# A hand-written scheduler's table of durations, and one PSUM ring for scores and sums: an attention, channel-mix and MLP kernel

## The chip, the cores and the metric

The kernel runs on one core of a Trainium2 chip. The metric is the device time of one execution in microseconds (us), lower is better. Three runs of the kernel before gave 2530.54, 2530.79 and 2534.72 us, median 2530.79. One further execution was recorded by the hardware profiler; all rows below are from that one.

## The reference

Three stages follow one another, all in float32 (cut to what matters):

```python
scores = (1 / S) * z @ z.T                  # per batch: B, S, D = 4, 3072, 256; z has 64 columns
x = u * (np.maximum(scores, 0) ** 2 @ v)
x_prev = x shifted by one row
r = sigmoid((mu_r * x + (1 - mu_r) * x_prev) @ w_r)
x = r * (np.maximum((mu_k * x + (1 - mu_k) * x_prev) @ w_k, 0) ** 2 @ w_v)
out = np.maximum(x @ w_in, 0) ** 2 @ w_out
```

The last line is the second MLP on the rows of the second stage. The change touches only the first stage, the attention.

## The kernel before, in words

The attention (`attention()`, L411 to L885) works in 24 blocks of 512 query columns, 6 per batch, numbered `n`; `ib` is the block's number in its batch. A block runs over 24 steps `s` of 128 keys, in 6 groups `g` of 4 steps. In each step TensorE multiplies the values (`vhl`, a high and a low part) with the squared scores (`ahi`, `alo`, again a high and a low part) and adds to four PSUM banks: two halves of 128 output rows (`d` = 0, 1), each kept in two banks because two matmuls of 64 rows run side by side (`attend_mm`, L678). A step is 12 matmuls.

The scores are symmetric. For `g >= ib` TensorE computes a pair of score tiles (`score_pair`, L581) into two PSUM banks; ScalarE takes relu into a tile `a` (L593) and squares it (L598); ScalarE or VectorE casts the high part (`high`, L615, the cast is in a helper at L240); VectorE subtracts for the low part (`low`, L622). For `g > ib` VectorE also transposes the tile in 32x32 blocks into `turn` (L556), and after four of them a DMA stores it (`store_turned`, L559). The blocks with `g < ib` load these stored tiles back (`load_turned_scores`, L568) instead of computing them. `spread[ib, g]` is true for `ib >= 2`: there the transpose writes and reads with another order of its axes.

At a block's end the four sums are copied out of PSUM (`gate`, L735): `gate_part` copies one bank into `x` (L716), `gate_rest` the other into `rest` or `a` (L721), `gate_add` adds them, `gate_mult` multiplies by the transposed `u` (`turn_u`, tile `uT`, one buffer for each `d`), and `gate_store` sends the product to DRAM (L733). The two last steps of a block do `d` = 0 first, and the first step of the next block begins with its `d` = 0, so that the first two banks have 1.36 us (two steps' `d` = 1 part) to be copied out. In between, TensorE also issues the score pairs of the steps up to seven ahead.

The order in which each engine gets its instructions is made on the host by `Plan` (L22 to L170), a list scheduler. Each operation is a node with an engine (P, V, S, D for TensorE, VectorE, ScalarE and DMA; some may go to S or V), a cost and what it depends on. TensorE's order is fixed, and it gives the due times: a node's due time is that of whoever depends on it, less a lag (L84 to L90). `run` then plays time forward: each engine takes, of the nodes that are ready and have their buffers, the one due first. Buffers are rings (`take` reserves one, `use` adds a reader); a buffer is free when the last reader has ended by the plan's own clock. `MARGIN` scales the costs for each engine, `lead` says how long before its due time a load may start. The chip does not see the plan's times: each engine works its queue in the planned order and waits on semaphores. A DMA is issued by SP's queue, which is also in order.

In the plan before, all DMA issues take 0.1 us of the queue (L151), a transpose of scores costs 0.63, and the first matmuls of a block name the copies of the last block's sums as their dependences (L698):

```python
before = get("acc", d) if s % NJ == 0 and 0 in terms else ()
...
i = on_pe(attend_mm, s, d, ks, deps=(x, *v_nodes(b, g, c // 2), *(before or ())), cost=0.2267 * len(ks))
```

Score tiles have a ring `w` of four PSUM banks, the sums four banks of their own (`ps_d`).

Of the kernel before, what the change touches and what calls it, by code (L numbers as in the profile page):

```python
# [8 lines left out]
F32 = mybir.dt.float32  # L9
# [12 lines left out]
class Plan:  # L22
# [6 lines left out]
    def __init__(self, **rings):  # L29
        self.nodes, self.takes, self.users_of, self.last = [], {}, {None: []}, {}  # L30
        self.held = {k: [None] * n for k, n in rings.items()}
        self.beside = {}
        self.place, self.tiles, self.turns, self.lines = {}, {}, dict.fromkeys(rings, 0), {}
# [28 lines left out]

    def load(self, f, *a, deps=(), cost=4.5, lead=1e9):
        return self.node("D", cost, lambda e: f(*a), *deps, lead=lead)

# [7 lines left out]
    def run(self, **free):  # L73
# [43 lines left out]
        while waiting or pe:  # L117
            best = None
            slots = [(i, t) for i in waiting if (t := slot(i)) is not None]
            for e in "PVSD":  # L120
                if e == "P":
                    cand = [(pe[-1], t)] if pe and not missing[pe[-1]] and (t := slot(pe[-1])) is not None else []
                else:
                    cand = [(i, t) for i, t in slots if e in nodes[i][0]]
                if not cand:
                    continue
                start = max(free[e], min(t for _, t in cand))
                rank = lambda i: nodes[i][4] + self.BEHIND_CASTS * (e + nodes[i][0] == "VSV")
                i = min((i for i, t in cand if t <= start), key=lambda i: (rank(i), i))
                if self.ahead and e in "VS":  # L130
                    end = start + self.cost_on(i, e) * self.MARGIN[e]
                    soon = [(rank(k), k, t) for k, t in cand if start < t < end - 0.1 and rank(k) < rank(i) - 1.0
                            and nodes[k][4] + late < end + self.ahead]
                    if soon:
                        first = min(t for _, _, t in soon)
                        fits = [k for k, t in cand if t <= start and start + self.cost_on(k, e) * self.MARGIN[e] <= first + 0.1]
                        if fits:
                            i = min(fits, key=lambda i: (rank(i), i))
                        else:
                            start = first  # L140
                            i = min((k for k, t in cand if t <= start), key=lambda i: (rank(i), i))
                if best is None or start < best[0]:
                    best = start, e, i
            start, e, i = best
            if e == "P":
                pe.pop()
                late = max(late, start - self.due_of[i])
            else:
                waiting.remove(i)
            took = self.cost_on(i, e) * self.MARGIN[e]  # L150
            free[e] = start + (took if e != "D" else 0.1)  # L151
            ended[i] = end = start + took
# [21 lines left out]
def tile_relu2_attention__rwkv_channel_mix__relu2_mlp(  # L174
# [236 lines left out]
    def attention():  # L411
        with ExitStack() as st:
# [3 lines left out]
            FIRST, LEAD, WHOLE = 4, 7, 2  # L416
            ps_s = st.enter_context(tc.tile_pool(name="ps_s", bufs=4, space=PSUM))
            ps_d = st.enter_context(tc.tile_pool(name="ps_d", bufs=1, space=PSUM))
            z_raw, zT, zz, zhi, zlo, vhl, uT = {}, {}, {}, {}, {}, {}, {}
            plan = Plan(a=4, hi=LEAD + 1, lo=LEAD + 1, w=4, zn=2, zT=1, turn=2, mixed=3, raw=3, vhl=NG, zz=NG // 2,  # L420
                        uT0=1, uT1=1, rest=1, e=1, m=1)
# [4 lines left out]
                          "lo": [io.tile([P, T], F32R, tag="alo", name="alo", bufs=LEAD + 1) for _ in range(LEAD + 1)],  # L426
                          "w": [ps_s.tile([P, T], F32, tag="w", name="sps") for _ in range(4)],
                          "zn": [io.tile([P, T], F32, tag="zn", name="zn") for _ in range(2)],
# [47 lines left out]
            def z_nodes(b, g):  # L476
# [3 lines left out]
                if b:  # L480
                    ready = take(load(load_z, b, g, cost=5.0, lead=60.0, deps=(get("zload"),)), "zn", key)
                    last["zload",] = ready
# [4 lines left out]
                else:  # L487
                    ready = last["zn", g] if g == 1 else take(load(load_z, b, g, cost=4.5, lead=14.0), "zn", key)
                    ready = take(use(on_pe(turn_z, b, g, deps=(ready,), cost=0.3), key), "w", ("zps", g))
# [24 lines left out]
            def v_nodes(b, g, h):  # L514
                if ("vn", b, g, h) in last:
                    return last["vn", b, g, h]
                if h == 0:
                    if b or g:
                        last["v", b, g] = take(load(load_v, b, g, cost=5.5, lead=40.0 if b else 14.0), "raw", ("v", b, g))
                        take(last["v", b, g], "vhl", ("vhl", b, g))  # L520
                    before = last["v", b, g]
                else:
                    before = v_nodes(b, g, 0)[0]
# [107 lines left out]
            def turned_nodes(n, g):  # L631
                key, b = ("ready", n, g), n // NB
                first = take(node("D", 0.01, lambda e: place_turned(n, g), last["stored", b, g, n % NB], lead=45.0),
                             "mixed" if n < NBLK - 1 else "zz", key)
                last[key] = [use(load(load_turned_scores, n, g, k, deps=(first,), cost=5.5), key) for k in range(R)]

            def scores(s):
# [27 lines left out]
                if g > ib:  # L665
                    key = "turn", b, ib, g
                    v_ = use(on_v(turn, s, ib, g, c, deps=(q, get(*key)), cost=0.63), ("rel", s))
                    plan.beside[v_] = last["at", s][1], 0.5
# [5 lines left out]
                    if c == G - 1:  # L674
                        reads = get("ready", (b - 1) * NB + g, ib) or ()
                        last["stored", b, ib, g] = use(load(store_turned, ib, g, deps=(v_, *reads), cost=5.5), key)

            def attend_mm(s, d, terms):  # L678
# [3 lines left out]
                if first and terms[0] == 0:  # L682
                    acc[n, d] = [ps_d.tile([P, T], F32, tag=f"v{d}{i}", name=f"v{d}") for i in range(2)]
                ds_ = slice(d * P, (d + 1) * P)
# [11 lines left out]
            def attend(s, d, terms):  # L696
                n, b, ib, g, c = chunk(s)
                before = get("acc", d) if s % NJ == 0 and 0 in terms else ()  # L698
                hi, lo = last["at", s]
                if s < WHOLE:  # L700
                    use(on_pe(attend_mm, s, d, terms, deps=(hi, last["v", 0, 0], *(before or ())), cost=0.85), ("whole", s), ("v", 0, 0))
                    return
                for part in ((0, 1), (2,)):
                    ks = tuple(k for k in terms if k in part)
                    if ks:
                        x, key = (lo, "lo") if 2 in part else (hi, "hi")
                        i = on_pe(attend_mm, s, d, ks, deps=(x, *v_nodes(b, g, c // 2), *(before or ())), cost=0.2267 * len(ks))
                        last["mm", d] = use(i, (key, s), ("vhl", b, g))

# [25 lines left out]
            def gate(n, d):  # L735
                ld = take(load(load_u, n, d, cost=4.5, lead=30.0), "zn", ("u", n, d))
                tr = take(use(on_v(turn_u, n, d, deps=(ld,), cost=0.63), ("u", n, d)), f"uT{d}", ("uT", n, d))
# [13 lines left out]
                last["mult", d] = last["mult", n, d] = m  # L751
                last["acc", d] = p, r
                last["xT", n, d] = use(load(gate_store, n, d, deps=(m,), cost=3.0), ("uT", n, d))

# [31 lines left out]
            last["zn", 1] = node("D", 5.0, lambda e: None)  # L786
            mu_loaded = load(load_mu, lead=100.0)
            om_made = on_v(make_om, deps=(mu_loaded,), cost=0.15)
# [40 lines left out]
            for i, (src, done, rests) in enumerate(conversions):  # L829
# [5 lines left out]
                k0, total = sum(ops[:i - mine[0]]), sum(ops)  # L835
                p = take(load(load_raw, key, src, src.shape[1], src.shape[2], cost=6.0, lead=8.0), "raw", key)
                for k, f in enumerate(convert(key, done, rests)):
# [34 lines left out]
            for k, (n, which, c) in enumerate([(n, w, c) for n in range(2) for w in range(2 - n) for c in range(ND)]):  # L872
                if (which, c) == (0, 0):
                    ld = load(load_x, n, deps=[*(last["xT", n, d] for d in range(ND)), *blends], lead=25.0)
                    blends = []
# [6 lines left out]
                use(on_v(mixed, n, which, c, True, deps=(hi,), due=due + 3), key)  # L882
            plan.MARGIN = {"P": 1.0, "V": 1.0, "S": 1.0, "D": 1.0}
            plan.ahead = 1.0
# [837 lines left out]
```

## Time and profile before

| what | value |
|---|---|
| median of three runs | 2530.79 us |
| the profiled execution | 2529.5 us |
| its span, first to last instruction | 2527.7 us |
| TensorE busy | 2474.2 us (98%) |
| VectorE busy | 2091.2 us (83%) |
| ScalarE busy | 1798.9 us (71%) |
| mean granted TensorE clock | 0.993 |
| end of the attention (last matmul on `vhl`) | about 984 us |

A busy engine is not one at its limit, so the idle stretches of TensorE are read next to its granted clock: a stretch with a clock of 0.5 costs twice the time for the same matmuls. A wait names the engine that waited, its line, and what ended the wait. In a timeline, a line stands for some instructions of one kind in a row; the bracket at its end is the idle time of that engine before it.

### The profile page before, as it was taken

The page shows a single profiled execution, that of the slowest core. Times are in us where ns is not written, and L with a number is a line of the kernel's source. Part 1 is how long each engine was busy: PE and PEld are TensorE (multiplying, and loading weights), DVE is VectorE, ACT ScalarE, POOL GpSimd, SP SyncE. Part 2 cuts the span into 40 slices and gives each one's busy share as a digit, 9 for nine tenths or more (in the row PEclk, how much of TensorE's full clock was granted, in tenths as well). Part 3 has the DMA queues.
Part 4 walks back from the last instruction along what each step waited for, and adds up shares of the span by engine and source line. Part 5 has one row for each costly group of instructions (what it writes and reads, how often), then busy time and mean ns, then how long its engine had stood idle before and what let it go on. Part 6 is the DMA issues. An engine that isn't in the chain of part 4 may idle for free.

```text
span 2527.7 us, 39583 instructions
## 1 busy us (share of the span) xinstructions
PE 2474.2 (98%) x14721; PEld 2044.2 (81%) x14721; DVE 2091.2 (83%) x3473; ACT 1798.9 (71%) x3266; POOL 0.7 (0%) x6
## 2 busy tenths in 40 slices
PE   9989999999999999999999999999999999999998
PEld 6878887788778778888888888888888888888887
DVE  8878887898788787999999998877777777777776
ACT  8756875686578666888888887666666666666665
POOL 0000000000000000000000000000000000000000
PEclk9999999999999999999999999999999999999999
DMA  8667566666657654232232211100110011100100
GB/s 221 180 192 197 179 196 177 170 196 197 190 160 216 187 162 138 80 104 80 82 106 80 88 67 59 34 17 17 34 34 17 17 34 34 30 22 17 34 17 18
DMA packets 309442, 257.95 MB, mean 102 GB/s; under 512 B 205312, under 2 KB 224768, under 8 KB 306176
## 3 DMA queue, kind: packets, MB, share of 16 engines
q1 hardware_dynamic: 307136, 254.89, 34.3%
q8 instruction: 115, 1.88, 0.3%
q10 hardware_dynamic: 2112, 0.52, 0.1%
q14 instruction: 79, 0.65, 0.1%
HBM read 149.45 MB, written 105.91 MB: 101 GB/s over the span
## 4 chain that ended last, share of the span: by engine, by line
PE 85%; DVE 6%; DMA 3%; ACT 2%; SPq 2%; issue 2%; DVEq 0%; ACTq 0%
PE ups L1135 26%; PE v L693 21%; PE v L1151 10%; PE v L1153 10%; PE v L1152 10%; PE ups L369 3%; PE sps L586 3%; DVE alo L622 3%; SPq L438 1%; DMA xT<-uT 1%; DVE turn L556 1%; ACT a L593 1%; ACT a L598 1%; DMA raw<-in_moe_w_v_dram 0%; SPq L573 0%
## 5 line engine op out<-in xcount | busy, mean ns | idle before, releaser
L693 PE MATMUL v<-ahi,vhl 64*128 64x512 f32 x4592 | 729.4, 392 | 28.9 <-DVE x L240 12.8
L693 PEld LDWEIGHTS v<-ahi,vhl 64*128 64x128 f32 x4592 | 525.2, 187 | 118.4 <-DVE x L240 17.3
L693 PE MATMUL v<-alo,vhl 64*128 64x512 f32 x2296 | 476.0, 392 | 9.1 <-DVE alo L622 9.0
L1172 ACT ACTIVATE s<-s 128x512 f32<-128x512 f32 x288 | 180.8, 628 | 324.2 <-DVE s L1167 324.2
L693 PEld LDWEIGHTS v<-alo,vhl 64*128 64x128 f32 x2296 | 301.0, 187 | 55.9 <-DVE alo L622 16.0
L1151 PE MATMUL v<-hhi,wout 128*128 128x512 f32 x768 | 299.0, 389 | 0.0
L1153 PE MATMUL v<-hlo,wout 128*128 128x512 f32 x768 | 299.0, 389 | 0.0
L1152 PE MATMUL v<-hhi,wout 128*128 128x512 f32 x768 | 299.0, 389 | 0.0
L1135 PE MATMUL ups<-d,win 128*128 128x512 f32 x1056 | 296.6, 389 | 0.0
L1184 DVE TENSOR_TENSOR hlo<-s,hhi 128x512 fp32r<-128x512 f32 x384 | 264.5, 689 | 16.5 <-ACT hhi L240 1.0
L593 ACT ACTIVATE a<-sps 128x512 f32<-128x512 f32 x335 | 192.8, 610 | 96.6 <-PE sps L586 47.0
L1176 ACT ACTIVATE s<-s 128x512 f32<-128x512 f32 x384 | 231.4, 628 | 6.1
L1167 DVE TENSOR_TENSOR s<-ups,su 128x512 f32<-128x512 f32 x192 | 131.4, 684 | 122.8 <-PE ups L1135 122.8
L1135 PEld LDWEIGHTS ups<-d,win 128*128 128x128 f32 x1056 | 198.3, 188 | 41.1
L1135 PE MATMUL ups<-b,win 128*128 128x512 f32 x792 | 222.4, 389 | 0.0
L556 DVE STREAM_TRANSPOSE turn<-a 128x512 f32<-128x512 f32 x240 | 206.0, 862 | 15.0 <-ACT a L598 7.8
L622 DVE TENSOR_TENSOR alo<-a,ahi 128x512 fp32r<-128x512 f32 x334 | 215.5, 677 | 2.5 <-ACT ahi L240 0.6
L598 ACT ACTIVATE a<-a 128x512 f32<-128x512 f32 x334 | 200.3, 646 | 0.0
L240 ACT CAST ahi<-mixed 128x512 fp32r<-128x512 f32 x220 | 132.9, 621 | 94.7 <-PE v L693 86.5
L586 PE MATMUL sps<-zz 64*128 64x512 f32 x1002 | 168.1, 393 | 7.5 <-ACT a L593 6.8
L1135 PEld LDWEIGHTS ups<-b,win 128*128 128x128 f32 x792 | 148.7, 188 | 30.8
L1151 PEld LDWEIGHTS v<-hhi,wout 128*128 128x128 f32 x768 | 144.2, 188 | 30.4
(209 smaller groups left out, 4287.6 us busy)
## 6 DMA issues: line engine op xcount, KB each, us to landing
turned<-turn SPq DMA_DIRECT2D x60, 1024.0 KB, 5.1
mixed<-turned SPq DMA_DIRECT2D x220, 256.0 KB, 4.9
zn<-in_u_dram SPq DMA_DIRECT2D x192, 64.0 KB, 3.5
xT<-uT SPq DMA_DIRECT2D x48, 256.0 KB, 2.8
x2d<-sig SPq DMA_DIRECT2D x48, 256.0 KB, 2.0
x<-x2d SPq DMA_DIRECT2D x12, 1024.0 KB, 4.8
out_dram<-y SPq DMA_DIRECT2D x94, 128.0 KB, 2.3
raw<-in_v_dram SPq DMA_DIRECT2D x23, 512.0 KB, 5.4
```

The source lines that it names most:

```text
L556: nc.vector.transpose(t[:, :, :, c, :], rel[s].rearrange("x (m r q) -> x q m r" if sp else "x (m q r) -> x q m r", m=G, q=R))
L586: nc.tensor.matmul(ps[i], lhsT=(zlo, zhi, zhi)[k][b, g][rows, (c + i) * P:(c + i + 1) * P], rhs=(zhi, zlo, zhi)[k][b, ib][rows], start=k = ...
L593: nc.scalar.activation(out=a, in_=ps_of.pop(s), func=AF.Relu, scale=1.0 / S)
L598: nc.scalar.activation(out=rel[s], in_=rel[s], func=AF.Square)
L622: nc.vector.tensor_tensor(out=lo, in0=a, in1=hi, op=ALU.subtract)
L693: nc.tensor.matmul(acc[n, d][i], lhsT=vt[rows, k % 2, c, ds_], rhs=at[s][k // 2][rows], start=first and k == 0, stop=fin and k == 2)
L1135: nc.tensor.matmul(ps, lhsT=weight(g, h, w), rhs=ops[g[0], j][y], start=first and m == 0, stop=m == 2, skip_group_check=not first)
L1151: nc.tensor.matmul(acc[p, b][d], lhsT=w[:, 0, c, ds_], rhs=hi, start=first, stop=False)
L1152: nc.tensor.matmul(acc[p, b][d], lhsT=w[:, 1, c, ds_], rhs=hi, start=False, stop=False)
L1153: nc.tensor.matmul(acc[p, b][d], lhsT=w[:, 0, c, ds_], rhs=lo, start=False, stop=last)
L1176: nc.scalar.activation(out=tmp[g, c], in_=tmp[g, c], func=AF.Square)
L1184: nc.vector.tensor_tensor(out=lo, in0=tmp.pop((g, c)), in1=hi, op=ALU.subtract)
```

## The change

Nothing that the chip computes is added or taken away. The change edits the plan's numbers and its PSUM rings:

- one ring `w` of eight banks for score tiles and sums; the first matmul of a block takes two of its banks for each `d`, and the copies `gate_part` and `gate_rest` are the banks' last readers. The dependence of that matmul on the copies of the block before is gone from the list of dependences; only the ring holds it back.
- a transpose of scores costs 1.02 where `spread` is true, 0.63 elsewhere.
- each load or store has an `issue` time that the DMA queue is taken for (0.1 by default; 0.5, 1.0 or 2.1 given), and other costs.
- the margins: V and S 1.03 instead of 1.0, D 1.6 instead of 1.0.

```diff
-    def load(self, f, *a, deps=(), cost=4.5, lead=1e9):
-        return self.node("D", cost, lambda e: f(*a), *deps, lead=lead)
+    def load(self, f, *a, deps=(), cost=4.5, lead=1e9, issue=0.1):
+        i = self.node("D", cost, lambda e: f(*a), *deps, lead=lead)
+        self.issue[i] = issue
+        return i
...
-            took = self.cost_on(i, e) * self.MARGIN[e]
-            free[e] = start + (took if e != "D" else 0.1)
+            took = self.cost_on(i, e) * (self.MARGIN[e] if e != "D" or i in self.issue else 1.0)
+            free[e] = start + (took if e != "D" else self.issue.get(i, 0.0))
...
-            ps_s = st.enter_context(tc.tile_pool(name="ps_s", bufs=4, space=PSUM))
-            ps_d = st.enter_context(tc.tile_pool(name="ps_d", bufs=1, space=PSUM))
+            ps_s = st.enter_context(tc.tile_pool(name="ps_s", bufs=8, space=PSUM))
...
-            plan = Plan(a=4, hi=LEAD + 1, lo=LEAD + 1, w=4, zn=2, zT=1, turn=2, mixed=3, raw=3, vhl=NG, zz=NG // 2,
+            plan = Plan(a=4, hi=LEAD + 1, lo=LEAD + 1, w=8, zn=2, zT=1, turn=2, mixed=3, raw=3, vhl=NG, zz=NG // 2,
...
-                    ready = take(load(load_z, b, g, cost=5.0, lead=60.0, deps=(get("zload"),)), "zn", key)
+                    ready = take(load(load_z, b, g, cost=6.0, lead=60.0, issue=2.1, deps=(get("zload"),)), "zn", key)
...
-                last[key] = [use(load(load_turned_scores, n, g, k, deps=(first,), cost=5.5), key) for k in range(R)]
+                last[key] = [use(load(load_turned_scores, n, g, k, deps=(first,), cost=6.0, issue=0.5), key) for k in range(R)]
...
-                    v_ = use(on_v(turn, s, ib, g, c, deps=(q, get(*key)), cost=0.63), ("rel", s))
+                    v_ = use(on_v(turn, s, ib, g, c, deps=(q, get(*key)), cost=1.02 if spread[ib, g] else 0.63), ("rel", s))
...
-                        last["stored", b, ib, g] = use(load(store_turned, ib, g, deps=(v_, *reads), cost=5.5), key)
+                        last["stored", b, ib, g] = use(load(store_turned, ib, g, deps=(v_, *reads), cost=6.5, issue=0.5), key)
...
-                    acc[n, d] = [ps_d.tile([P, T], F32, tag=f"v{d}{i}", name=f"v{d}") for i in range(2)]
+                    acc[n, d] = [place.pop(("acc", n, d, i)) for i in range(2)]
...
-                before = get("acc", d) if s % NJ == 0 and 0 in terms else ()
+                opens, banks = s % NJ == 0 and 0 in terms, [("acc", n, d, i) for i in range(2)]
+
+                def mm(ks, deps, cost):
+                    i = on_pe(attend_mm, s, d, ks, deps=deps, cost=cost)
+                    for k in banks:
+                        if opens and ks[0] == 0:
+                            take(i, "w", k)
+                        else:
+                            use(i, k)
+                    return i
...
-                ld = take(load(load_u, n, d, cost=4.5, lead=30.0), "zn", ("u", n, d))
+                ld = take(load(load_u, n, d, cost=6.0, lead=30.0, issue=2.1), "zn", ("u", n, d))
...
-                last["acc", d] = p, r
-                last["xT", n, d] = use(load(gate_store, n, d, deps=(m,), cost=3.0), ("uT", n, d))
+                use(p, ("acc", n, d, 1))
+                use(r, ("acc", n, d, 0))
+                last["xT", n, d] = use(load(gate_store, n, d, deps=(m,), cost=4.0, issue=0.5), ("uT", n, d))
...
-            plan.MARGIN = {"P": 1.0, "V": 1.0, "S": 1.0, "D": 1.0}
+            plan.MARGIN = {"P": 1.0, "V": 1.03, "S": 1.03, "D": 1.6}
             plan.ahead = 1.0
             plan.run(P=5.7, V=7.0, S=6.3, D=3.0)
```

The other loads (`load_v`, `load_raw` of the weights, `load_x`, the first `load_z`) get new costs and issue times in the same way.

## Rows read from the trace of the kernel before

**Rows 1.** Page, part 1: busy us, share of the span, instructions.

```profile
PE   2474.2 (98%) x14721; PEld 2044.2 (81%) x14721; DVE 2091.2 (83%) x3473; ACT 1798.9 (71%) x3266; POOL 0.7 (0%) x6
```

**Rows 2.** Windows: attention and the rest; columns as the first line says.

```profile
core 0: us, PE busy (x) PEld busy (x) DVE busy (x) ACT busy (x) POOL busy (x), PEclk, DMA share, GB/s
0.00:984.00 984.00, 936.82 (x7941) 771.44 (x7941) 817.34 (x1371) 679.29 (x1262) 0.70 (x6) 0.98 0.66 186
984.00:2527.70 1543.70, 1537.38 (x6781) 1272.74 (x6780) 1273.88 (x2103) 1119.65 (x2004) 0.00 (x0) 1.00 0.15 49
```

**Rows 3.** Waits of TensorE: us in total, times, longest us.

```profile
PE v L693 <- DVE x L240: 12.8, 10, 2.0
PE v L693 <- ACT rest L240: 10.7, 3, 5.4
PE v L693 <- DVE alo L622: 9.0, 11, 2.9
PE sps L586 <- ACT a L593: 6.8, 5, 2.9
PE v L693 <- ACT a L240: 2.4, 2, 1.5
PE v L693 <- DVE ahi L240: 2.4, 2, 1.5
...
PE v L693 <- DVE part L240: 0.5, 1, 0.5
```

**Rows 4.** Cores, then windows around three waits: granted clock in column PEclk.

```profile
core 0: 2527.7 us, clock 0.993
...
467.00:475.00 8.00, 7.58 (x45) 5.82 (x47) 7.09 (x12) 4.55 (x9) 0.00 (x0) 0.70 0.65 157
...
646.00:650.00 4.00, 3.92 (x21) 2.92 (x23) 3.97 (x9) 3.41 (x7) 0.00 (x0) 0.58 0.13 45
...
404.00:411.00 7.00, 6.52 (x31) 5.09 (x33) 6.63 (x10) 7.00 (x15) 0.00 (x0) 0.54 0.00 0
```

**Rows 5.** Timeline of TensorE at two block openings: start, us, instruction [idle before].

```profile
467.21 0.79 PE L693 MATMUL v<-ahi,vhl 64*128 64x512 f32 x1 [5.40 <-ACT rest L240]
...
869.50 0.73 PE L693 MATMUL v<-ahi,vhl 64*128 64x512 f32 x3 [2.00 <-DVE x L240]
```

**Rows 6.** Timelines of VectorE and ScalarE before the same two openings.

```profile
462.24 1.25 DVE L622 TENSOR_TENSOR alo<-a,ahi 128x512 fp32r<-128x512 f32 x2
...
466.58 0.57 ACT L240 COPY rest<-v 128x512 f32<-128x512 f32 x1
...
865.15 3.69 DVE L622 TENSOR_TENSOR alo<-mixed,ahi 128x512 fp32r<-128x512 f32 x6
868.76 0.68 DVE L240 COPY x<-v 128x512 f32<-128x512 f32 x1
```

**Rows 7.** VectorE's transposes of scores: the line's durations, one of each kind.

```profile
L556 DVE STREAM_TRANSPOSE turn<-a x240: 659/708/1143, 15.1 to 942.6; 128x512 f32<-128x512 f32 x120
...
53.27 0.70 DVE L556 STREAM_TRANSPOSE turn<-a 128x512 f32<-128x512 f32 x1
...
853.63 2.07 DVE L556 STREAM_TRANSPOSE turn<-a 128x512 f32<-128x512 f32 x2
```

**Rows 8.** VectorE waiting for DMAs: waits in total, and one case on three engines.

```profile
DVE uT L541 <- DMA xT<-uT: 43.2, 15, 7.4
...
642.08 0.71 DVE L541 STREAM_TRANSPOSE uT<-zn 128x512 f32<-128x512 f32 x1 [7.41 <-DMA xT<-uT]
...
646.12 1.20 ACT L593 ACTIVATE a<-sps 128x512 f32<-128x512 f32 x2 [9.37 <-DVE alo L622]
...
646.08 1.22 PE L693 MATMUL v<-alo,vhl 64*128 64x512 f32 x4 [2.86 <-DVE alo L622]
```

**Rows 9.** SP's queue: issues of the transposing loads and the store's landing time.

```profile
L438 SPq DMA_DIRECT2D zn<-in_u_dram x192: 311/487/3605, 25.8 to 954.2; - x192
...
L733 SPq DMA_DIRECT2D xT<-uT x48: 319/380/1517, 61.0 to 986.7; - x48
...
DMA to landing us min/median/max: 2.0/2.8/8.7
```

**Rows 10.** Timeline of TensorE: score pairs that waited for a PSUM bank.

```profile
404.48 1.27 PE L586 MATMUL sps<-zz 64*128 64x512 f32 x2 [2.86 <-ACT a L593]
...
851.35 0.97 PE L586 MATMUL sps<-zz 64*128 64x512 f32 x5 [0.42 <-ACT a L593]
```

More of the change, by code (lines that the diff above doesn't have):

```diff
@@ L31, in __init__ @@
         self.held = {k: [None] * n for k, n in rings.items()}
-        self.beside = {}
+        self.beside, self.issue = {}, {}
         self.place, self.tiles, self.turns, self.lines = {}, {}, dict.fromkeys(rings, 0), {}
@@ L426, in attention @@
                           "lo": [io.tile([P, T], F32R, tag="alo", name="alo", bufs=LEAD + 1) for _ in range(LEAD + 1)],
-                          "w": [ps_s.tile([P, T], F32, tag="w", name="sps") for _ in range(4)],
+                          "w": [ps_s.tile([P, T], F32, tag="w", name="sps") for _ in range(8)],
                           "zn": [io.tile([P, T], F32, tag="zn", name="zn") for _ in range(2)],
@@ L487, in z_nodes @@
                 else:
-                    ready = last["zn", g] if g == 1 else take(load(load_z, b, g, cost=4.5, lead=14.0), "zn", key)
+                    ready = last["zn", g] if g == 1 else take(load(load_z, b, g, cost=5.0, lead=14.0, issue=1.0), "zn", key)
                     ready = take(use(on_pe(turn_z, b, g, deps=(ready,), cost=0.3), key), "w", ("zps", g))
@@ L518, in v_nodes @@
                     if b or g:
-                        last["v", b, g] = take(load(load_v, b, g, cost=5.5, lead=40.0 if b else 14.0), "raw", ("v", b, g))
+                        last["v", b, g] = take(load(load_v, b, g, cost=6.0, issue=0.5, lead=40.0 if b else 14.0), "raw", ("v", b, g))
                         take(last["v", b, g], "vhl", ("vhl", b, g))
@@ L697, in attend @@
                 n, b, ib, g, c = chunk(s)
-                before = get("acc", d) if s % NJ == 0 and 0 in terms else ()
+                opens, banks = s % NJ == 0 and 0 in terms, [("acc", n, d, i) for i in range(2)]
[7 more added lines that the diff above has]
+                    return i
                 hi, lo = last["at", s]
                 if s < WHOLE:
-                    use(on_pe(attend_mm, s, d, terms, deps=(hi, last["v", 0, 0], *(before or ())), cost=0.85), ("whole", s), ("v", 0, 0))
+                    use(mm(terms, (hi, last["v", 0, 0]), 0.85), ("whole", s), ("v", 0, 0))
                     return
@@ L706, in attend @@
                         x, key = (lo, "lo") if 2 in part else (hi, "hi")
-                        i = on_pe(attend_mm, s, d, ks, deps=(x, *v_nodes(b, g, c // 2), *(before or ())), cost=0.2267 * len(ks))
-                        last["mm", d] = use(i, (key, s), ("vhl", b, g))
+                        last["mm", d] = use(mm(ks, (x, *v_nodes(b, g, c // 2)), 0.2267 * len(ks)), (key, s), ("vhl", b, g))
             def scratch_of(n, d):
@@ L786, in attention @@
             last["zn", 1] = node("D", 5.0, lambda e: None)
-            mu_loaded = load(load_mu, lead=100.0)
+            mu_loaded = load(load_mu, lead=100.0, issue=1.0)
             om_made = on_v(make_om, deps=(mu_loaded,), cost=0.15)
@@ L835, in attention @@
                 k0, total = sum(ops[:i - mine[0]]), sum(ops)
-                p = take(load(load_raw, key, src, src.shape[1], src.shape[2], cost=6.0, lead=8.0), "raw", key)
+                p = take(load(load_raw, key, src, src.shape[1], src.shape[2], cost=7.5, lead=8.0, issue=0.5), "raw", key)
                 for k, f in enumerate(convert(key, done, rests)):
@@ L873, in attention @@
                 if (which, c) == (0, 0):
-                    ld = load(load_x, n, deps=[*(last["xT", n, d] for d in range(ND)), *blends], lead=25.0)
+                    ld = load(load_x, n, deps=[*(last["xT", n, d] for d in range(ND)), *blends], cost=5.0, lead=25.0, issue=0.5)
                     blends = []
```

## The prediction, made before the changed kernel was run

> **What bounds the kernel now.** The page's busy shares come first [rows 1]: TensorE is busy for 98% of the span, so the time is its work plus its few idle stretches, at the granted clock. The windows say where the idle time lies [rows 2]: up to 984 us, where the attention ends, TensorE is busy for 936.8 us of 984.0, idle for 47.2; in the other 1543.7 us it is idle for 6.3 and the clock reads 1.00. The change edits only the attention's plan, so at most these 47.2 us, and what the lower clock costs, can be won. The clock reads 0.993 over the span [rows 4]: 0.7% of 2527.7 us is 17.7 us of lost pulses, all before 984 us [rows 2]. Some of them fall into idle time; in three stretches shown it reads 0.70 of 8 us, 0.58 of 4 and 0.54 of 7 [rows 4], 2.4, 1.7 and 3.2 us lost, each at or just behind a long wait of TensorE. So I count some 14 of the 17.7 as real, and the most that can be won is 47 + 14 = 61 us.
>
> The list of TensorE's waits sorts the 47 us [rows 3]. Waits on `x`, `rest`, `a` and `part` are block openings that wait until the last block's sums are copied out: 12.8 + 10.7 + 2.4 + 0.5 = 26.4 us in 16 waits. Waits on `alo`, `ahi` and of the score pairs on relu add 9.0 + 2.4 + 6.8 = 18.2. What is left, some 2 us, is the start.
>
> **Part by part.** The engines execute the same instructions before and after; only order, the choice of engine for a cast, and PSUM banks change. Each part is therefore a wait that goes or comes.
>
> *Openings.* At 869.50 TensorE waited 2.00 us for VectorE's copy of a sum [rows 5]. VectorE was late because it first did six low parts in 3.69 us, then the copy [rows 6]; the operands that the new block needs were among the six, done long before. With eight banks in one ring and no score pairs in flight there, four banks are free, and the block can open at once: 2.0 goes to 0. At 467.21 the wait was 5.40 us, for a ScalarE copy that began at 466.58 [rows 5, 6]. The low parts of the first two steps were done about 463.5 (1.25 us from 462.24), so with free banks TensorE could have started there, and not at 461.8 where it stopped: 3.7 of the 5.4 go, 1.7 stay. The same holds at every opening of `ib` = 3, 4 and 5, where no score pairs are in flight; by the timeline these are 24 of the 26.4 us. For `ib` = 1 (2.4 us) score pairs are in flight. I take 18 of 26.4 as saved, ends 8 (half of the 5.40 kind and some of the 2.0 kind come back as waits for operands) and 26.
>
> *Durations of the transposes.* The row gives 708 ns as the median of 240 and 1143 as the longest; a single one in block 1 takes 0.70, two in a block with `spread` 2.07 together [rows 7]. Six of the 15 stored pairs of a batch have `spread`, so 96 transposes cost 0.4 us more than the plan thinks, 38 us of VectorE that it fills with other work (casts of high parts, weight conversions). This is where VectorE is late before the openings above and where `alo` waits of up to 0.94 us come. In such a stretch two steps and a score pair give TensorE 3.4 us of work, while VectorE has two transposes at 1.03, two low parts at 0.62 and one cast at 0.3, 3.6 in all: with the true cost the plan can move the cast to ScalarE (71% busy), and no more. I take 1 us of some 6 that are not due to DMAs; ends 0 and 4.
>
> *DMA costs and issue times.* VectorE stood 43.2 us behind the store of `uT`, 15 times [rows 8]. The plan before thinks the store lands after 3.0 us and a queue slot costs 0.1; it lands after 2.8 as a median, 8.7 at worst, and each of the four issues of a `u` load takes 0.49 [rows 9], so a load's four take about 2 us. The transpose of the next `u` is not urgent, but the plan puts it right behind the store, and VectorE's queue then stops. At 642.08 it stood 7.41 us, ScalarE 9.37 behind it, and TensorE lost 2.86 [rows 8]; at 404.48 a score pair lost 2.86 in the same way [rows 10]. By the timeline three such places cost TensorE 11 us. With 4.0 x 1.6 = 6.4 us planned for the store, the transpose is put behind other work. I take 7; ends 2 and 11. The loads have enough lead (30 to 60 us) for their longer planned times; what is planned later is only the work that reads them.
>
> *Clock.* If the long waits go, their low stretches go: 8 of the 14; ends 3 and 13.
>
> *What the change adds.* The copies of the sums lose their due time. Before, the opening matmul depended on them, and they were due at once; now they are due only by `gate_mult` and the next block's scratch, one chain of copy, add and multiply (some 2.3 us in the plan) for each block back from the end, so that for most blocks ScalarE and VectorE take anything else that is ready first. The copies run when one of the two is idle in the plan (ScalarE is idle for 305 of 984 us, VectorE for 167 [rows 2]), so I expect a delay of a few us, not of a block. It matters where score pairs need banks: openings of `ib` = 0 (three) and 1 (four). There four old sums, four new ones and the pairs want eight banks. TensorE's queue is in order: behind a waiting opening or pair stand all later matmuls, and ScalarE and VectorE run dry behind those. The nearest rows are waits of a score pair for a bank, 0.42 and 2.86 us [rows 10]: seven openings cost 3 to 20 us. A gain below zero is left out, since the waits of score pairs in the present trace are already counted above. I take 7, 1 for each opening, nearer to the small row, because these openings don't wait on a stalled VectorE.
>
> The Trainium skill (PSUM — Partial Sum Buffer, section Summary: rules for kernel authors) tells the author to evacuate PSUM promptly because it is small. It speaks against this part; by it, the sum would go by the upper end, 20 instead of 7, and the gain would be 14, the time 2517. The trace agrees as far as it shows waits for these copies [rows 3].
>
> The sum: 18 + 1 + 7 + 8 - 7 = 27 us. From the profiled execution's 2529.5 (span 2527.7 and 1.8 around it) this gives 2502.5; the median shown is 1.3 above that execution, so 2504.
>
> **Rivals.** *VectorE takes over.* Without the openings' waits TensorE asks for low parts sooner, and VectorE, busy for 817 of 984 us, is what ends the wait. For it: in the `spread` stretch it has 3.6 us of work against TensorE's 3.4. Against it: after most openings come loaded scores, where VectorE's share is one low part for each step. Then only the 2.0 kind of openings half, and the DMA waits, are won: 6 + 7 + 4 - 5 = 12, time 2519.
>
> *Redistribution.* The list scheduler's order shifts as a whole, and new places with a late DMA or a late copy replace the old ones one for one: 2531.
>
> *The copies starve.* This is the slower side: openings of `ib` = 0, 1 and 2 (eleven) find ScalarE and VectorE busy with scores that are due first, the old sums stay in four banks, and score pairs run on what is left, each waiting for the relu of the pair before. Price: 2.9 us [rows 10] and 1.7 of clock [rows 4] for each opening, 51 us in all, against the 34 of the sum above without its last term: 17 slower, 2548. At 4.6 us each, it decides from the eighth of the eleven openings on (34 / 4.6 = 7.4). For it: nothing makes these copies urgent any more. Against it: the idle shares above.
>
> *The clock falls from changing banks.* In the present trace the clock falls only at seven places, all at long waits, though score tiles change between four banks all the time. The Trainium skill (TensorE: Matmul & The Clock Gate, section A second HAM failure mode: psum-queue depth-cycling) reports a kernel whose clock swung because it went through PSUM banks in turn with short idle times. No row here shows that without a long wait. If every one of 23 openings lost 1.7 us [rows 4], it would be 39 - 27 = 12 slower, 2543.
>
> **How the numbers follow.** Chances: the forecast 0.62 (2484 to 2516, all faster), VectorE takes over 0.14 (2512 to 2525, faster), redistribution 0.10, starving copies 0.12, bank clock 0.02. A measurement of this kernel tells a change of about 0.2%, 5 us, from none. So faster 0.76, same 0.10, slower 0.14. The lower bound takes saved openings 24, transposes 2, DMA 9, clock 12 and a cost of 3: 44 less than 2529.5, and 1.3 on top, so 2486, opened to 2484. The upper bound takes in redistribution with its 0.2%, up to 2534, and leaves out the slower cases, 0.14.
>
> **What would show it.** In the profile after: the waits of TensorE on `x`, `rest` and `a` fall from 26.4 to under 10 us; VectorE's wait for the store of `uT` falls from 43.2 to under 15; the clock rises from 0.993 to 0.996 or more; the attention ends near 957. Waits of `sps` on relu, or of openings on the copies, at the first two blocks of a batch, would show the starving copies; more `alo` waits VectorE's bound. The forecast is wrong if the busy TensorE time before the end of the attention grows, or if the idle time only changes its names.

## The result: 75 us faster, and the profile after

The changed kernel takes 2455.74 us (median of 4, 2455.14 to 2464.07) against 2530.66 before: ratio 0.971, 95% interval 0.969 to 0.974. That is 75 us, where 27 had been forecast with a range that ended at 2484. The profiled execution took 2456.03 us, with a span of 2454.2.

The windows of the changed kernel, attention and the rest (columns as in [rows 2]):

```profile
core 0: us, PE busy (x) PEld busy (x) DVE busy (x) ACT busy (x) POOL busy (x), PEclk, DMA share, GB/s
0.00:911.00 911.00, 907.22 (x7941) 811.64 (x7941) 803.00 (x1320) 706.59 (x1313) 0.70 (x6) 1.00 0.72 201
911.00:2454.20 1543.20, 1537.25 (x6782) 1272.61 (x6780) 1273.87 (x2103) 1119.84 (x2004) 0.00 (x0) 1.00 0.15 49
```

All of the gain is in the attention, which ends at 911 us, not 984; the rest takes 1543 us as before. TensorE's idle time there fell from 47.2 to 3.8 us, and the clock column reads 1.00, not 0.98. Its waits, all of them (us in total, times, longest; lines have moved by one or two, so L694 is L693 of before, and the sums now sit in tiles called `sps`):

```profile
PE sps L694 <- DVE alo L623: 1.9, 1, 1.9
PE sps L790 <- PEq L1717: 0.8, 1, 0.8
PE sps L579 <- ACT zT L465: 0.7, 1, 0.7
PE sps L587 <- DVE zz L469: 0.2, 1, 0.2
PE sps L460 <- DMA zn<-in_z_dram: 0.2, 1, 0.2
```

Everything in [rows 3] is gone but one wait on `alo`; the other four are the start. VectorE's waits for DMAs are smaller, not gone:

```profile
DVE uT L542 <- DMA xT<-uT: 17.7, 9, 4.0
DVE uT L542 <- DMA mixed<-turned: 8.1, 3, 4.4
DVE uT L542 <- DMA zn<-in_u_dram: 6.6, 2, 6.3
```

The first answers 43.2 us in 15 waits [rows 8].

Idle time and clock don't add up to the gain. TensorE's idle time fell by 43 us. The lower clock lost 17.1 us of pulses before (seven stretches, the sum of (1 - granted clock) x length up to 984 us), of which 2.8 fall into idle time: 14 real. Together 58 of the 73 us by which the attention became shorter. The other 15 lie inside TensorE's busy time, which fell by 29.6 us (936.8 to 907.2) with the same 7941 matmuls, twice the clock's 14. What they are is answered by a list that the prediction did not read, the waits of TensorE's weight loader (PEld). In the kernel before:

```profile
PEld v L693 <- DVE x L240: 17.3, 11, 2.5
PEld v L693 <- DVE alo L622: 16.0, 20, 3.3
PEld v L693 <- ACT rest L240: 12.5, 4, 5.8
PEld sps L586 <- ACT a L593: 11.1, 12, 3.3
PEld v L693 <- ACT a L240: 3.4, 3, 1.9
PEld v L693 <- DVE ahi L240: 3.2, 2, 2.0
```

The same causes as in [rows 3], but 63.5 us in 52 waits in place of 44.1 in 33. All its waits add up to 75.2 us before and 12.2 after; of the 12.2, 9.5 lie in the first 33 us and 2.3 are the wait on `alo`. The matmuls run as overlapping pairs: 24 of them take 2.72 us, so a pair starts every 0.227 us, but a matmul's row lasts 0.39. When the next operand is late, the engine is shown busy until the last row ends, and a wait shorter than that does not show at all. PEld has no such tail, as its rows last 0.18.

### The profile page after: what moved, and what is told of

Read it like the earlier page. It is cut to its first block, busy times and chain, and to the rows that moved or that the text cites. A ratio compares the mean times of both kernels' runs of the same rounds, so it can differ in the third digit from the quotient of the medians.

```text
span 2454.2 us, 39676 instructions
## 1 busy us (share of the span) xinstructions
PE 2444.5 (100%) x14721; PEld 2084.2 (85%) x14721; DVE 2076.9 (85%) x3422; ACT 1826.4 (74%) x3317; POOL 0.7 (0%) x6
## 4 chain that ended last, share of the span: by engine, by line
PE 97%; DMA 1%; DVE 1%; SPq 0%; issue 0%; ACT 0%; DVEq 0%
PE sps L694 30%; PE ups L1146 27%; PE v L1164 10%; PE v L1163 10%; PE v L1162 10%; PE sps L587 4%; PE ups L371 4%; DMA mixed<-turned 1%; DVE turn L557 0%; DMA zn<-in_z_dram 0%; DVE alo L623 0%; PE v L393 0%; PE v L390 0%; PE v L392 0%; PE sps L460 0%
## 5 line engine op out<-in xcount | busy, mean ns | idle before, releaser
L694 PE MATMUL sps<-ahi,vhl 64*128 64x512 f32 x4592 | 649.7, 386 | 0.0
L694 PEld LDWEIGHTS sps<-ahi,vhl 64*128 64x128 f32 x4592 | 479.0, 184 | 51.2 <-issue 0.2
L694 PE MATMUL sps<-alo,vhl 64*128 64x512 f32 x2296 | 389.9, 386 | 1.9 <-DVE alo L623 1.9
L694 PEld LDWEIGHTS sps<-alo,vhl 64*128 64x128 f32 x2296 | 244.1, 184 | 27.9 <-DVE alo L623 2.3
L1146 PEld LDWEIGHTS ups<-d,win 128*128 128x128 f32 x1056 | 198.3, 188 | 41.1
L1164 PEld LDWEIGHTS v<-hlo,wout 128*128 128x128 f32 x768 | 144.2, 188 | 29.8
```

The costliest lines, as they stand in the source:

```text
L694: nc.tensor.matmul(acc[n, d][i], lhsT=vt[rows, k % 2, c, ds_], rhs=at[s][k // 2][rows], start=first and k == 0, stop=fin and k == 2)
L1146: nc.tensor.matmul(ps, lhsT=weight(g, h, w), rhs=ops[g[0], j][y], start=first and m == 0, stop=m == 2, skip_group_check=not first)
L1164: nc.tensor.matmul(acc[p, b][d], lhsT=w[:, 0, c, ds_], rhs=lo, start=False, stop=last)
```

## The experiments

Fourteen kernels, the two and twelve more. All times below are medians; those of the kernel before, taken beside them in three rounds, are 2529.6 to 2532.5 us, so a difference of some 3 us between two rows can be nothing. Each ratio is to the kernel before of the same round.

| kernel | us | ratio to before (95%) |
|---|---|---|
| changed kernel | 2455.7 | 0.971 (0.969 to 0.974) |
| `ring_only` | 2535.5 | 1.0027 (1.0016 to 1.0038) |
| `ring_due` | 2517.9 | 0.994 (0.993 to 0.996) |
| `turn_only` | 2525.8 | 0.998 (0.997 to 0.999) |
| `store_only` | 2506.5 | 0.990 (0.988 to 0.992) |
| `dma_only` | 2486.2 | 0.982 (0.981 to 0.984) |
| `table_only` | 2473.5 | 0.978 (0.977 to 0.980) |
| `old_dma` | 2498.7 | 0.989 (0.987 to 0.991) |
| `old_margin` | 2480.9 | 0.980 (0.978 to 0.982) |
| `margin_2` | 2476.0 | 0.978 (0.977 to 0.980) |
| `old_turn` | 2470.6 | 0.977 (0.975 to 0.978) |
| `copies_due` | 2459.0 | 0.971 (0.970 to 0.973) |
| `old_vs` | 2458.7 | 0.971 (0.970 to 0.973) |

**The ring alone.** All numbers of the plan as before, the eight banks as in the change.

```diff
-            ps_s = st.enter_context(tc.tile_pool(name="ps_s", bufs=4, space=PSUM))
-            ps_d = st.enter_context(tc.tile_pool(name="ps_d", bufs=1, space=PSUM))
+            ps_s = st.enter_context(tc.tile_pool(name="ps_s", bufs=8, space=PSUM))
...
-                before = get("acc", d) if s % NJ == 0 and 0 in terms else ()
+                opens, banks = s % NJ == 0 and 0 in terms, [("acc", n, d, i) for i in range(2)]
```

> The kernel before with the ring of eight PSUM banks alone; all durations, issue times and margins as before. If the ring is what gave the time (the block openings, 26.4 us of TensorE's idle time and the low clock behind them): 2480 to 2495 us, TensorE's waits on x, rest and a under 5 us, VectorE's wait of 43 us for the store of uT still there. If the table of durations gave it: 2515 to 2535, the openings' waits gone but waits on alo and of score pairs in their place.

Measured: 2535.5, 0.3% slower than before and just above the second range. TensorE's waits, the five longest, then what VectorE waits for:

```profile
PE sps L587 <- ACT a L594: 16.6, 10, 4.4
PE sps L694 <- DVE alo L623: 12.2, 12, 4.0
PE sps L694 <- DVE ahi L242: 11.0, 3, 3.8
PE sps L694 <- ACT ahi L242: 2.4, 1, 2.4
PE sps L587 <- ACT x L242: 2.1, 1, 2.1
...
DVE uT L542 <- DMA xT<-uT: 58.2, 20, 7.0
```

The ring does what it says: openings no longer wait on `x`, `rest` or `a` (26.4 us before, 2.1 now, and that is a score pair waiting for a copy). The idle sum is the same, 46.4 us for 47.2: waits of score pairs and on operands have come in place of the openings'. By this run alone the openings would be only where TensorE met a lateness of VectorE. But the edit also takes the due time from the copies, and `ring_due`, below, shows that this part of it costs 18 us.

**The table alone.** All new numbers, with the banks and the dependence of before.

```diff
-            ps_s = st.enter_context(tc.tile_pool(name="ps_s", bufs=8, space=PSUM))
+            ps_s = st.enter_context(tc.tile_pool(name="ps_s", bufs=4, space=PSUM))
+            ps_d = st.enter_context(tc.tile_pool(name="ps_d", bufs=1, space=PSUM))
...
-                opens, banks = s % NJ == 0 and 0 in terms, [("acc", n, d, i) for i in range(2)]
+                before = get("acc", d) if s % NJ == 0 and 0 in terms else ()
```

> The changed kernel with the PSUM banks of before (four for scores, four for sums, the openings again dependent on the copies); all new durations, issue times and margins kept. If the table gave most of the time: 2465 to 2485 us, the waits on alo and of score pairs gone, openings still waiting some 10 us in all. If the ring gave most: 2500 to 2520, openings still some 25 us.

Measured: 2473.5, as the first range had it, so 56 us of the 75 without the ring. TensorE's waits:

```profile
PE v L695 <- DVE x L242: 4.9, 3, 3.2
PE v L695 <- ACT rest L242: 4.5, 2, 2.7
PE v L695 <- ACT a L242: 3.8, 1, 3.8
```

Half of the openings' waits (13.2 of 26.4 us) went with the banks left as they were, and the waits on `alo`, `ahi` and of score pairs went wholly. On top of the table the ring is worth 18 us (2473.5 to 2455.7): these openings' waits and the low clock behind them.

**Parts of the table.** Each kernel below is the changed one with one part undone, or the one before with one part done.

In `old_turn`:

```diff
-                    v_ = use(on_v(turn, s, ib, g, c, deps=(q, get(*key)), cost=1.02 if spread[ib, g] else 0.63), ("rel", s))
+                    v_ = use(on_v(turn, s, ib, g, c, deps=(q, get(*key)), cost=0.63), ("rel", s))
```

In `old_dma` all loads and stores have their costs of before, each issue 0.1, and:

```diff
-            free[e] = start + (took if e != "D" else self.issue.get(i, 0.0))
+            free[e] = start + (took if e != "D" else 0.1)
...
-            plan.MARGIN = {"P": 1.0, "V": 1.03, "S": 1.03, "D": 1.6}
+            plan.MARGIN = {"P": 1.0, "V": 1.03, "S": 1.03, "D": 1.0}
```

> The changed kernel with 0.63 for every transpose of scores. If VectorE is the tight engine where the stored tiles have the other order of axes, some 96 x 0.4 us of its work are again not planned: alo waits come back in the third and fourth block of each batch, 2465 to 2480 us. If the other parts leave it enough slack: within 5 us of 2455.7.

> The changed kernel with the old costs of loads and stores, 0.1 us for each issue and margin 1.0 for DMAs. If waits of VectorE for DMAs were a main cause: VectorE's wait for the store of uT is back near 40 us, TensorE loses 11 us and some clock, 2468 to 2485. If the eight banks let TensorE run past them: within 5 us of 2455.7.

Measured: 2470.6 and 2498.7. The DMA numbers are worth 43 us in the changed kernel, beyond the 12 to 29 expected, the transposes 15. Without the DMA numbers VectorE's waits are back, and the eight banks don't let TensorE run past them; the first row is the wait of [rows 8], the last the waits of score pairs for a bank:

```profile
DVE uT L542 <- DMA xT<-uT: 46.8, 12, 10.5
DVE e L284 <- DMA raw<-in_moe_w_k_dram: 14.0, 4, 8.3
DVE e L284 <- DMA raw<-in_moe_w_out_dram: 11.6, 2, 6.2
...
PE sps L587 <- ACT a L594: 10.5, 10, 2.3
```

With the transposes at 0.63 it is `alo` that is late, in seven waits. By the timeline five of them are near the end of a batch's fourth block and two in its fifth; the third, also expected, has none. VectorE itself also stands longer behind loads of stored scores (third row; 8.1 us in the changed kernel), so the 15 us are not only the transposes' own length:

```profile
PE sps L694 <- DVE alo L623: 5.0, 7, 1.2
PE sps L587 <- ACT a L594: 2.4, 3, 1.0
...
DVE uT L542 <- DMA mixed<-turned: 29.0, 5, 8.4
```

The same two parts alone, on the kernel before:

> The kernel before with the new DMA numbers alone (costs, issue times, margin 1.6). If the parts add up (table 56 us, of which the transposes some 15): 2480 to 2495 us. If the true costs of the transposes are needed before the DMA numbers help: 2500 to 2515. In both, VectorE's wait for the store of uT falls under 30 us and openings still wait over 10.

> The kernel before with 1.02 for the transposes with the other order of axes, and nothing else. If 38 us of VectorE's work that was not planned are a cause of their own: 2510 to 2522. If VectorE's DMA waits hide it: 2525 to 2535.

Measured: 2486.2 and 2525.8. The DMA numbers give 44 us alone, the transposes 5 alone and 13 with the DMA numbers (2486.2 to 2473.5; the margins of V and S, which moved the changed kernel by 3, are in that step too). The opening waits on VectorE (12.8 us on `x` before) even grow with either part alone; with both, in `table_only`, 4.9 are left, and the ring takes away the rest. TensorE's first row in `dma_only` and in `turn_only`:

```profile
PE v L695 <- DVE x L242: 18.9, 10, 3.4
```

```profile
PE v L695 <- DVE x L242: 19.5, 9, 4.2
```

**One number.** The kernel before with the store planned at 6.4 us.

```diff
-                last["xT", n, d] = use(load(gate_store, n, d, deps=(m,), cost=3.0), ("uT", n, d))
+                last["xT", n, d] = use(load(gate_store, n, d, deps=(m,), cost=6.4), ("uT", n, d))
```

> The kernel before with one number changed: the store of uT is planned at 6.4 us instead of 3.0. If VectorE standing behind this store is the largest single cause: its wait of 43 us falls under 20, and the time to 2495 to 2515. If it is one of many waits that replace each other: 2522 to 2535.

Measured: 2506.5, 24 to 26 us for one number. VectorE's longest waits there:

```profile
DVE e L282 <- DMA raw<-in_moe_w_in_dram: 16.3, 4, 7.6
DVE e L282 <- DMA raw<-in_moe_w_k_dram: 15.8, 3, 6.6
DVE e L282 <- DMA raw<-in_moe_w_out_dram: 13.7, 3, 6.2
```

The wait for the store has left the list (1.5 us, once). Others have grown: the first step of a weight conversion (L282) waited 34.6 us over the whole attention before and waits 61 here. These loads, too, were planned too short (6.0 us; medians of 5.9 to 7.7 in the trace of before). That the rest of the DMA numbers, another 20 us, lie in such places is likely but was not taken apart.

The 3.0 was not wrong as the store's landing time, whose median is 2.8 [rows 9]. VectorE's next transpose waits for more than that: from the end of the product (L729) to the landing of its store the trace of before has a median of 5.3 us, over 3.0 in 36 of 48 cases and 15.1 at most, since the store first stands in SP's queue, for 1.9 us as a median.

All waits of VectorE for DMAs in the attention, added up from the traces, are 117 us before, 89 in `store_only` and 35 in `dma_only`. So 28 us less gave 24 us of time, and 82 less gave 44.

**How much slack for DMAs.**

The edit of `old_margin`; `margin_2` has 2.0 in the same place.

```diff
-            plan.MARGIN = {"P": 1.0, "V": 1.03, "S": 1.03, "D": 1.6}
+            plan.MARGIN = {"P": 1.0, "V": 1.03, "S": 1.03, "D": 1.0}
```

> The changed kernel with the DMA margin at 1.0 instead of 1.6; new costs (store 4.0, loads 5.0 to 7.5) and issue times kept. If the slack of the margin is what keeps VectorE from waiting for DMAs: 2475 to 2495 us, VectorE's waits for DMAs near those with all old DMA numbers. If issue times and costs did it: within 6 us of 2455.7.

> The changed kernel with DMA margin 2.0 instead of 1.6. If slack for DMAs is all that counts, no worse than 2455.7 + 3, with VectorE's wait for the store of uT under 15 us. If planned DMA times can be too long (buffers held longer, loads planned late): 2462 to 2475.

Measured: 2480.9 with 1.0 and 2476.0 with 2.0, so both are 20 to 25 us worse than 1.6. With 1.0 the wait for the store is back (41.7 us, 14 times), and all waits of VectorE for DMAs are 76 us, between the 33 of the changed kernel and the 123 of `old_dma`. With 2.0 they are the shortest of all kernels, 17 us, nearly all of it the store's, and another wait has come, of score pairs for the split parts of z:

```profile
DVE uT L542 <- DMA xT<-uT: 16.1, 6, 5.4
...
PE sps L587 <- DVE zz L469: 9.4, 4, 4.2
```

In these four places the last part of z had landed 5 to 8 us before VectorE's transpose of it began, and VectorE was busy with other work until then: the transpose stood late in its queue, and the data was there. That the plan put it there because it took the loads of z for longer than they are is argued: no run changed these loads alone. Of the 43 us of the DMA numbers, then, some 25 are the margin (2480.9 to 2455.7) and 18 the costs and issue times (2498.7 to 2480.9); the two latter were not separated.

**The due time of the copies.** It is given back without the dependence, on the changed kernel and on the ring alone.

```diff
                         if opens and ks[0] == 0:
                             take(i, "w", k)
+                            for x in get("acc", d) or ():
+                                plan.beside[x] = i, -0.2
...
+                last["acc", d] = p, r
                 use(p, ("acc", n, d, 1))
```

> The changed kernel, with the due time of the copies given back: each copy of a sum is due 0.2 us before the next block's opening matmul, which still depends on the ring alone. If the lost due time costs nothing (the copies find idle time anyway): within 4 us of 2455.7. If it hid a loss: faster by up to 2, no more, since TensorE is idle for 3.8 us only. If early copies push other work of ScalarE and VectorE back: 2460 to 2470.

> The ring of eight alone (old durations), with the due time of the copies given back in the same way. If the ring alone was slow because its copies starve: 2505 to 2520 us, TensorE's waits of score pairs for a bank from 16.6 to under 8. If it was slow because VectorE stands behind DMAs whatever the ring: 2525 to 2540, as without the due time, and VectorE's wait for the store of uT stays over 40 us.

Measured: 2459.0 (3 us slower than the changed kernel) and 2517.9 (18 us faster than the ring alone, and 13 to 15 faster than the kernel before). In the changed kernel the lost due time costs nothing that can be told from none. With the old table it costs 18 us; score pairs waiting for relu fall from 16.6 to 7.4 us, TensorE's idle time from 46.4 to 35.3:

```profile
PE sps L694 <- DVE alo L623: 10.7, 13, 4.0
PE sps L694 <- DVE ahi L242: 8.9, 3, 3.3
PE sps L587 <- ACT a L594: 7.4, 5, 2.8
...
DVE uT L542 <- DMA xT<-uT: 50.7, 14, 7.2
```

The copies are late in the changed kernel too. At the end of each of the first three batches one of a block's four sums waits long for its copy; at the first of them, in `ring_only` and then in the changed kernel, the block's last matmuls and this copy:

```profile
260.87 0.39 PE L694 MATMUL sps<-alo,vhl 64*128 64x512 f32 x2
279.83 0.60 ACT L242 COPY a<-sps 128x512 f32<-128x512 f32 x1
```

```profile
237.26 0.39 PE L694 MATMUL sps<-alo,vhl 64*128 64x512 f32 x2
253.88 0.65 DVE L242 COPY a<-sps 128x512 f32<-128x512 f32 x1
```

The bank is held for some 19 us in the one and 17 in the other. With the due time the last copy ends at most 6.6 us (`ring_due`) and 3.4 us (`copies_due`) after its block. So a late copy costs time under the old table and none under the new; by which of its late copies `ring_only` lost the 18 us was not followed. `ring_due` has a sign of both expectations: the time and the score pairs fell as the first had it, and the wait for the store stayed over 40 as the second had it.

**Margins of VectorE and ScalarE.** The changed kernel with 1.0 in place of 1.03.

> The changed kernel with margin 1.0 for VectorE and ScalarE. If 3% matters: 2465 to 2475. If not, within 5 us of 2455.7; this also shows how much a schedule that is only shuffled moves the time.

Measured: 2458.7, with TensorE idle for 4.2 us. If this is taken for an order that is only shuffled, that moves the time by about 3 us, and the 3 us of `copies_due` can't be told from it.

**The loss and the two lists.** For all kernels, up to the end of the attention: its end, TensorE's idle time, the sum of the weight loader's waits over 0.15 us, the pulses lost to the lower clock (without those in idle time), and what is left of the end after taking off the clock and one of the two. All are worked out in this way from the trace of one execution of each kernel (in `table_only` one that was 5 us above the median).

| kernel | end | idle | PEld waits | clock | end - idle - clock | end - PEld - clock |
|---|---|---|---|---|---|---|
| before | 984.1 | 47.2 | 75.2 | 14.3 | 922.6 | 894.6 |
| `ring_only` | 988.8 | 46.4 | 75.4 | 17.9 | 924.5 | 895.5 |
| `turn_only` | 978.4 | 41.1 | 61.4 | 19.3 | 918.0 | 897.7 |
| `ring_due` | 972.0 | 35.3 | 64.3 | 11.7 | 925.0 | 896.0 |
| `store_only` | 961.4 | 32.8 | 55.3 | 8.8 | 919.8 | 897.3 |
| `old_dma` | 951.4 | 22.8 | 47.2 | 6.4 | 922.2 | 897.8 |
| `dma_only` | 944.3 | 26.3 | 41.5 | 5.1 | 912.9 | 897.7 |
| `old_margin` | 939.9 | 14.9 | 35.4 | 4.8 | 920.2 | 899.7 |
| `table_only` | 933.8 | 15.1 | 27.9 | 8.4 | 910.3 | 897.5 |
| `margin_2` | 931.3 | 14.8 | 28.2 | 4.2 | 912.3 | 898.9 |
| `old_turn` | 924.4 | 9.5 | 24.3 | 1.7 | 913.2 | 898.4 |
| `copies_due` | 914.8 | 5.0 | 14.2 | 1.7 | 908.1 | 898.9 |
| `old_vs` | 912.8 | 4.2 | 12.6 | 1.7 | 906.9 | 898.5 |
| changed | 911.1 | 3.8 | 12.2 | 0.0 | 907.3 | 898.9 |

The last column is the same within 5 us for schedules whose ends differ by 78; the one before it varies by 18. So the loss of TensorE is what its weight loader waits, plus the clock, and the changed kernel's attention is at the limit that TensorE's matmuls set (by estimate 7941 at a pair each 0.227 us, about 900 us), plus some 10 us of start.

## Why the prediction was wrong, point by point

The direction held, and the store, the openings and the transposes were each worth time, as the prediction had it. The step that failed is the term of the DMA costs and issue times, put at 7 us with ends of 2 and 11: it measured 43. Other terms were mis-sized too, and the ceiling above them all was too low.

*"The most that can be won is 47 + 14 = 61 us."* This failed: the attention alone became 73 us shorter. The clock's 14 is right and is all gone. The 47 are TensorE's idle time, which leaves out the tail of the last matmul in each wait and all waits shorter than it. By the weight loader's list the ceiling would have been 75.2 + 14.3, less the 12 that stayed, 77; measured 73.

*Openings, 18 of 26.4, ends 8 and 26.* All 26.4 are gone, and with eight banks a block does open at once: no opening in `ring_only` or `ring_due` waits for a copy. In `ring_due` that gains 13 to 15 us, within the ends; a part comes back as waits on operands, as the prediction feared ("VectorE takes over": 21.1 us on `alo` and `ahi`, 11.4 before). In `ring_only` the copies without a due time took it all away. But the waits were not only a cost of having four banks: in `table_only` half of them go without the ring. Over the right table the ring is worth 18 us.

*Durations of the transposes, 1 us, ends 0 and 4.* Measured 5 alone and 15 in the changed kernel. The 38 us of unplanned work were counted, and then priced only by the waits on `alo`. The plan's whole order rests on them: six low parts ahead of a copy [rows 6] may be such an order, made in the belief that there was time; that is argued, not shown.

*DMA costs and issue times, 7 us, ends 2 and 11.* The mis-sized term: 43 us in the changed kernel, 44 alone. The mechanism was right: planned longer, the store no longer stops VectorE, and this one number gave 24 us back. The size was not. The prediction followed VectorE's 43.2 us behind the store to three places where a late `alo` or score pair ended at TensorE, 11 us, and put the rest at nothing without a reason. It also left out VectorE's other waits for DMAs, 74 of 117 us, 34.6 of them before weight conversions. All this is lateness of everything behind it in VectorE's queue, and VectorE is busy for 817 of 984 us. It ends in waits with other names: the DMA numbers alone took away most of the waits on `alo` and of score pairs and 9 of the 14 us of clock. By the sums above, a us less of VectorE's standing behind DMAs was worth from a half (44 for 82) to nearly all (24 for 28) of itself, where 7 for 43 had been put.

*Clock, 8 of 14, ends 3 and 13.* All 14. The low stretches went with the long waits, as the prediction had it, though the table shows them not in step (8.4 us lost in `table_only` with 15 idle, 6.4 in `old_dma` with 23).

*What the change adds, 7 us, ends 3 and 20.* Nothing could be measured in the whole change: `copies_due` is no faster. The rule of the Trainium skill (PSUM — Partial Sum Buffer, section Summary: rules for kernel authors), evacuate promptly, is not contradicted by this. `ring_due` against `ring_only` shows a price of 18 us, near the upper end of this term, under the old table. In the changed kernel a sum can stay in its bank for 17 us after its block and nothing waits for it.

*The rivals.* "The copies starve" holds for the ring alone, in the direction and to a size of 18 us. In the whole change some copies are as late and cost nothing. "The clock falls from changing banks" did not happen: the sums go round eight banks, and up to 911 us the clock reads 1.00. In `ring_only`, with the same banks, it is at half, the lower of its two levels, in nine stretches, each at or just behind a wait of TensorE of 2.1 us or more. So the case in the Trainium skill (TensorE: Matmul & The Clock Gate, section A second HAM failure mode: psum-queue depth-cycling), short idle times between groups of matmuls, is not met here; TensorE is idle for 3.8 us in 911.

*The signs in the profile.* Openings under 10 us: 0. Wait for the store under 15: 17.7, a near miss. Clock 0.996 or more: 0.999. End of the attention near 957: 911.

The terms were added as if independent. They are not: the ring is worth -6 us alone, 16 over the DMA numbers (margins of V and S included) and 18 over the table; the transposes 5 alone and 15 last.

## What to carry to other kernels

Take TensorE's loss from the weight loader's waits, not from the idle time of matmuls that overlap. Where a host-side scheduler orders in-order queues, compare each of its durations with the trace first, and for a DMA from the end of the work before it to its landing, the queue included: here that was 5.3 us where the plan had 3.0 and the landing alone took 2.8. A wrong one can cost a half or more of what its engine stands still, spread over waits that carry other names. Before a wait is called the price of a missing buffer, ask whether its releaser was late for another reason: half of the openings' waits went without more banks. And ask what the buffer's edit does to the order besides: here a lost due time hid what the ring gave.

## What the runs showed of the hardware

Two of the transfers that VectorE waits for did not get faster; they got slower, and the kernel gained. The page's DMA issues (count, KB each, median us to landing) of the loads of stored scores and the stores of `uT`, before and then after:

```profile
mixed<-turned SPq DMA_DIRECT2D x220, 256.0 KB, 4.9
...
xT<-uT SPq DMA_DIRECT2D x48, 256.0 KB, 2.8
```

```profile
mixed<-turned SPq DMA_DIRECT2D x220, 256.0 KB, 6.6
...
xT<-uT SPq DMA_DIRECT2D x48, 256.0 KB, 5.3
```

Not all did: the loads of v went from 5.4 to 4.8 us, the stores of turned scores from 5.1 to 5.0. The same bytes move in 911 us and not in 984, at 201 GB/s and not 186 [rows 2]. Whether the denser traffic or the other order of issues made the two slower is not shown. Either way, a plan that goes by the medians of the slower run is too short for the faster one that it makes; that a margin of 1.6 over its costs did better than 1.0 agrees with this.

VectorE's 32x32 block transpose of 128x512 takes 0.66 to 0.71 us in one order of axes and 1.05 to 1.14 in the other, `spread`, on the same shape: its time depends on the order in which it reads and writes.
